# Attention and a max-out feed-forward on one core: the head of the loop's table in another order

## The chip, the cores and the metric

The kernel runs on one core of a Trainium2 chip. A core has five engines that work side by side, each with a queue that it goes through in order: TensorE (PE in the profile, with PEld for its weight loads), VectorE (DVE), ScalarE (ACT), GpSimd (POOL) and SyncE (SP), which here only issues DMAs. The metric is the device time of one execution in microseconds (us), as the median of several runs. Before the change it is 288.52 us.

## What is computed

```python
scores = scale * (q @ k_all.T)        # k_all: 16 beacon keys, then 576 keys; per batch and head
scores = where(causal, -1e9, scores)  # beacons are always seen
a = exp(scores - max); a /= a.sum(-1) + 1e-9
x = (a @ v_all), heads side by side   # 8 batches x 576 tokens = 4608 rows of 512
h = maximum(maximum(x @ w1, x @ w2), x @ w3)   # 512 -> 768
out = h @ w_out                                # 768 -> 512
```

There are 8 batches and 8 heads of width 64. Inputs and outputs are float32; the kernel computes its matmuls in bfloat16.

## The kernel before

**The work.** Heads go in pairs: pair p (0 to 31) is two heads of batch p // 4. Two pairs are a quad (0 to 15), and a half of a quad's 288 queries is one step of values. For a pair, q and k are loaded in float32 (a stage "st", one of eight), cast to bfloat16 (`cast`, tile p16), and turned so that the head dimension lies on the partitions (qT and kT, six of each). Pairs 10 to 13 are turned by PE (`pair`: twelve matmuls of line 393 into PSUM, then DVE moves kT, line 459, and ACT or DVE moves qT, line 448, in this order). Pairs from 14 on are turned by a transposing DMA (`cross`, line 374, on SP's queue). `keys` puts the 16 beacon keys in front of kT (line 455).

A pair's scores are four groups (0 to 3) of matmuls (line 509), each in one PSUM place of two banks. ACT takes the exp of a group into the tile at_sb (line 524), and `mask` sets what the causal order forbids to zero: on POOL with a select (line 543), on DVE with a product by a triangle (line 541). `("scores", p, g, n)` emits matmuls and exp, with n spare matmuls on constants first (line 473, 320 columns each); `("score", p, g)` emits the matmuls alone and `("exp", p, g)` the exp later.

`values` of a quad and a half multiplies the exps by ones (the sums) and by V (line 584) into two banks. `invert` is Ln and Exp on ACT (lines 604 and 606), and `multiply` is three products on DVE (line 616) into xT. V is loaded by batch in two pieces and cast by POOL (`cast v`, line 311).

The feed-forward is a list of units in order: for each block of 512 tokens 18 units of four matmuls (lines 646, or 665 for halves of block 0) with a cast or max by DVE (lines 654, 656, 673, 675), then four units of six matmuls for the output (line 682) that DVE copies to y (line 694). `("ffn 1", bank)` emits the next unit into a bank, `("ffn 2",)` the next two into a place of the ring.

**PSUM.** Eight banks: pv0 and pv1, one bank each, and a ring of three places of two banks, two called sc and one called wide. Each user of the ring (a group of scores, values "ring", "ffn 2", "ffn 1" with "ring", a pair that PE turns) takes the next place in turn, and PE has to wait until the user three turns ago has been read by DVE or ACT.

**The order.** Nothing is scheduled by a planner: two tables, `first_steps` and `loop_steps`, list the steps, and each engine does its part of them in the table's order. The loop's head works on pairs 8 to 13 (values 3 to 5) and on the end of block 0 and block 1 of the feed-forward. `("load", n)` issues the next n loads of a list (after pair 15: V of batch 3 in two pieces, the beacon keys of batches 4 to 7, pairs 16 to 19, V of batch 4, and so on); with an engine's name, that engine first writes one element of the stage, so that the load waits for its place in that engine's queue. `late` gives up the tiles of the start and sets up the nine y tiles. The change touches the table `loop_steps` alone. What a bank's name means to `values` is decided so:

```python
banks = None
if bank == "ring": ...      # values(): the next ring place
elif bank == "ffn": ...     # two ffn banks
else:                       # any other name
    banks = [pv_bank(i, [128, 512], FP32) for i in range(2)]
```

Of the kernel before, what the change touches and what calls it, by code (L numbers as in the profile page):

```python
# [16 lines left out]
def kernel(  # L17
# [141 lines left out]
    ring = [(sc_psum, "sc"), (sc_psum, "sc")]  # L159
# [684 lines left out]
    def start_late():  # L844
# [226 lines left out]
        ("mask", 6, 2, "pool"),  # L1071
    ]
    loop_steps = [
        ("late",),
        ("ffn 1", "pv1"),
        ("scores", 8, 1, 0),
        ("scores", 8, 0, 0),
        ("score", 8, 2),
        ("values", 3, 0, "pv"),
        ("invert",),  # L1080
        ("exp", 8, 2),
        ("values", 3, 1, "ring"),
        ("mask", 8, 1, "pool"),
        ("mask", 8, 0, "pool"),
        ("mask", 8, 2, "pool"),
        ("multiply",),
        ("invert",),
        ("multiply",),
        ("ffn 2",),
        ("ffn 1", "pv0"),  # L1090
        ("cast", 10, "pool", "pool"),
        ("load", 1),
        ("ffn 1", "pv1"),
        ("ffn 1", "pv0"),
        ("scores", 8, 3, 0),
        ("scores", 9, 0, 0),
        ("scores", 9, 1, 0),
        ("mask", 8, 3, "pool"),
        ("mask", 9, 0, "pool"),
        ("mask", 9, 1, "pool"),  # L1100
        ("ffn 1", "pv1"),
        ("ffn 1", "pv0"),
        ("pair", 10, "act"),
        ("keys", 10, "act"),
        ("ffn 2",),
        ("ffn 1", "pv1"),
        ("cast", 11, "pool", "pool"),
        ("load", 1),
        ("cast v", 2, 0),
        ("load", 1),  # L1110
        ("scores", 9, 2, 0),
        ("scores", 9, 3, 0),
        ("mask", 9, 2, "pool"),
        ("mask", 9, 3, "pool"),
        ("ffn 1", "pv0"),
        ("ffn 1", "pv1"),
        ("pair", 11, "act"),
        ("keys", 11, "act"),
        ("ffn 1", "pv0"),
        ("cast v", 2, 1),  # L1120
        ("load", 1),
        ("ffn 1", "pv1"),
        ("scores", 10, 1, 0),
        ("scores", 10, 0, 0),
        ("score", 10, 2),
        ("values", 4, 0, "pv"),
        ("invert",),
        ("exp", 10, 2),
        ("values", 4, 1, "ring"),
        ("mask", 10, 1, "pool"),  # L1130
        ("mask", 10, 0, "pool"),
        ("mask", 10, 2, "pool"),
        ("multiply",),
        ("invert",),
        ("multiply",),
        ("ffn 2",),
        ("ffn 1", "pv0"),
        ("cast", 12, "pool", "pool"),
        ("load", 1),
        ("cast", 14, "pool", "pool"),  # L1140
        ("load", 1),
        ("ffn 1", "pv1"),
        ("scores", 10, 3, 0),
        ("scores", 11, 0, 0),
        ("scores", 11, 1, 0),
        ("mask", 10, 3, "pool"),
        ("mask", 11, 0, "pool"),
        ("mask", 11, 1, "pool"),
        ("ffn 1", "pv0"),
        ("cast keys 2", "pool"),  # L1150
        ("cross", 14, 0),
        ("cross", 14, 1),
        ("cast", 15, "pool", "pool"),
        ("load", 1),
        ("pair", 12, "act"),
        ("keys", 12, "act"),
        ("ffn 2",),
        ("ffn 1", "pv1"),
        ("cast", 13, "pool", "pool"),
        ("load", 1),  # L1160
        ("scores", 11, 2, 0),
        ("scores", 11, 3, 0),
        ("mask", 11, 2, "pool"),
# [14 lines left out]
        ("values", 5, 1, "ring"),  # L1178
        ("mask", 12, 1, "pool"),
        ("mask", 12, 0, "pool"),  # L1180
        ("mask", 12, 2, "pool"),
        ("multiply",),
        ("invert",),
# [2 lines left out]
        ("ffn 1", "pv0"),  # L1186
        ("cast", 16, "pool", "pool"),
        ("ffn 1", "pv1"),
        ("scores", 12, 3, 0),
        ("scores", 13, 0, 0),  # L1190
        ("scores", 13, 1, 0),
# [478 lines left out]
```

## Time and profile before

| what | us |
|---|---|
| median of 3 runs (lowest to highest) | 288.52 (288.41 to 289.38) |
| the profiled execution, its own time | 288.88 |
| its span, first to last instruction | 287.1 |
| busy: PE, DVE, ACT, POOL | 278.4, 169.7, 143.8, 121.6 |

The granted TensorE clock is 0.997 of full speed over the span. A row of a time line gives the start in us, the length in us, the engine, the kernel's line, the operation, output tile <- input tiles with shapes, and xN for N instructions taken together; in square brackets stands how long the engine had been idle and what ended that. A row of the groups by shape gives, behind the bar, the busy time in us and the mean time of one in ns, then the idle time before them. A row of the table of stretches gives the stretch, its length, and the busy time of PE, PEld, DVE, ACT and POOL with their instructions, the granted clock, the share of the DMA engines and GB/s. Matmuls overlap, so a matmul's length is longer than its step to the next.

### The profile page before, as it was taken

The numbers are of one execution on the slowest core, as the hardware profiler recorded it, in microseconds if no ns is written. First come the engines' busy times: TensorE is split into PE (matmuls) and PEld (weight loads), VectorE is DVE, ScalarE is ACT, GpSimd is POOL, SyncE is SP. The second block draws the span as 40 slices with busy tenths as digits, with TensorE's granted clock in tenths as the row PEclk, the third lists the DMA queues.
The fourth block names the chain that finished last, engine by engine and source line by source line (L and its number), as shares of the span: only waits on it lengthen the run. The fifth ranks groups of instructions, "written<-read, shape, count | busy, mean of one in ns | idle before, by whom it ended". The sixth has DMA issues, their size and how long they took to land.

```text
span 287.1 us, 8822 instructions
## 1 busy us (share of the span) xinstructions
PE 278.4 (97%) x3706; PEld 160.2 (56%) x3731; DVE 169.7 (59%) x317; ACT 143.8 (50%) x242; POOL 121.6 (42%) x252
## 2 busy tenths in 40 slices
PE   8999999999999999999999999999999999999994
PEld 7656777754646454545456787445544545444442
DVE  2456878766575657465745755567466655373372
ACT  3876676835647564736483268444853452201200
POOL 4562327736484584737376446653633230000000
PEclk9999999999999999999999999999999999999998
DMA  8999998999999987999999989999983003002104
GB/s 154 174 166 209 222 245 158 244 204 211 191 158 159 172 118 134 195 176 184 184 229 191 194 170 221 222 168 177 189 323 123 2 2 148 0 0 107 41 0 147
DMA packets 118231, 45.30 MB, mean 158 GB/s; under 512 B 107312, under 2 KB 112944, under 8 KB 118192
## 3 DMA queue, kind: packets, MB, share of 16 engines
q1 hardware_dynamic: 111984, 39.20, 74.7%
q0 software_dynamic: 5648, 5.21, 11.8%
q8 instruction: 29, 0.48, 0.7%
q10 hardware_dynamic: 560, 0.33, 0.5%
q14 instruction: 10, 0.08, 0.1%
HBM read 35.13 MB, written 9.44 MB: 155 GB/s over the span
## 4 chain that ended last, share of the span: by engine, by line
PE 89%; ACT 3%; DMA 2%; DVE 2%; POOL 1%; issue 1%; ACTq 0%; POOLq 0%
PE pv L646 21%; PE sc L646 15%; PE wide L646 8%; PE pv L682 6%; PE sc L509 6%; PE sc L682 5%; PE wide L682 4%; PE pv L584 4%; PE wide L584 4%; PE sc L584 4%; DMA quad<-in_k_dram 2%; PE wide L509 2%; ACT at_sb L524 2%; PE pv L473 2%; PE sc L665 1%; PE pv L665 1%
## 5 line engine op out<-in xcount | busy, mean ns | idle before, releaser
L524 ACT ACTIVATE at_sb<-sc 128x736 bf16<-128x736 f32 (+5 forms) x95 | 79.4, 868 | 59.2 <-PE sc L509 58.6
L543 POOL TENSOR_SCALAR_AFFINE_SELECT at_sb<-at_sb 128x256 bf16<-128x256 bf16 (+2 forms) x143 | 52.4, 385 | 109.3 <-ACT at_sb L524 101.2
L646 PEld LDWEIGHTS <-w_sb 128*128 128x128 bf16 x648 | 61.1, 98 | 60.7 <-issue 4.9
L646 PE MATMUL pv<-xT,w_sb 128*128 128x512 bf16 (+1 forms) x315 | 65.3, 347 | 0.3
L646 PE MATMUL sc<-xT,w_sb 128*128 128x512 bf16 (+1 forms) x205 | 45.6, 363 | 0.7 <-issue 0.2
L656 DVE TENSOR_TENSOR hT<-hT,pv 128x512 bf16<-128x512 bf16 x48 | 32.4, 686 | 13.2 <-PE pv L646 13.2
L524 ACT ACTIVATE at_sb<-wide 128x736 bf16<-128x736 f32 (+3 forms) x33 | 27.7, 840 | 23.6 <-PE wide L509 23.5
L255 POOL CAST p<-st 96x768 bf16<-96x768 f32 x48 | 38.2, 825 | 0.0
L682 PEld LDWEIGHTS <-hT 128*128 128x128 bf16 x210 | 19.5, 98 | 23.5 <-issue 1.1
L616 DVE TENSOR_TENSOR xT<-pv,recip 128x288 bf16<-128x288 f32 (+2 forms) x48 | 14.2, 351 | 26.4 <-ACT recip L606 26.3
L509 PE MATMUL sc<-qT,kT 64*128 64x288 bf16 (+6 forms) x298 | 27.8, 277 | 1.6 <-DVE kT L443 0.7
L656 DVE TENSOR_TENSOR hT<-hT,sc 128x1024 bf16<-128x1024 bf16 (+1 forms) x19 | 20.8, 1104 | 12.6 <-PE sc L646 12.5
L509 PEld LDWEIGHTS <-kT 64*128 64x128 bf16 x400 | 14.6, 94 | 20.8 <-issue 13.0
L584 PEld LDWEIGHTS <-v_sb 128*32 128x32 bf16 (+1 forms) x1408 | 24.8, 96 | 1.7 <-issue 0.6
L646 PE MATMUL wide<-xT,w_sb 128*128 128x512 bf16 (+1 forms) x110 | 24.5, 364 | 0.1
L682 PE MATMUL pv<-w_out_sb,hT 128*128 128x512 bf16 x83 | 19.9, 380 | 0.1
L311 POOL CAST v_sb<-st 128x1536 bf16<-128x1536 f32 (+2 forms) x21 | 18.4, 897 | 0.0
L654 DVE CAST hT<-pv 128x512 bf16<-128x512 f32 x20 | 13.7, 688 | 5.0 <-PE pv L646 5.0
L682 PE MATMUL sc<-w_out_sb,hT 128*128 128x512 bf16 x68 | 16.3, 380 | 0.2
L665 PEld LDWEIGHTS <-w_sb 128*128 128x128 bf16 x144 | 13.0, 98 | 3.4 <-issue 1.4
L606 ACT ACTIVATE recip<-lnd 128x288 f32<-128x288 f32 x32 | 14.2, 443 | 1.0
L694 DVE COPY y<-pv 128x512 f32<-128x512 f32 x14 | 9.7, 692 | 8.4 <-PE pv L682 8.1
(119 smaller groups left out, 278.8 us busy)
## 6 DMA issues: line engine op xcount, KB each, us to landing
st<-in_q_dram SPq DMA_DIRECT2D x24, 288.0 KB, 5.2
st<-in_k_dram SPq DMA_DIRECT2D x24, 288.0 KB, 6.3
st<-in_v_dram SPq DMA_DIRECT2D x24, 256.0 KB, 5.5
out_dram<-y SPq DMA_DIRECT2D x9, 512.0 KB, 3.8
out_dram<-y SPq DMA_DIRECT2D x17, 256.0 KB, 4.1
w_sb<-in_moe_w_dram POOLq DMA_DIRECT2D x6, 384.0 KB, 8.7
st<-in_v_dram SPq DMA_DIRECT2D x8, 224.0 KB, 4.9
st<-in_v_dram SPq DMA_DIRECT2D x8, 160.0 KB, 4.8
```

The costliest lines, as they stand in the source:

```text
L255: cast(t16.rearrange("p r h d -> p h r d"), st[0:QP, i * NQ2 : (i + 1) * NQ2].rearrange("p (h r d) -> p h r d", h=2, r=QR),)
L311: cast(v_sb[0:n, t:t1].rearrange("p t h d -> p (t h d)"), st[0:n, (t - t_lo) * H * D : (t1 - t_lo) * H * D],)
L509: nc.tensor.matmul(ps[:, e, off : off + q1 - q0], kT[hs, 128 * t : 128 * t + 128], qT[hs, q0:q1], start=True, stop=True, tile_position=(64 ...
L524: nc.scalar.activation(out=both_heads(p, gi), in_=ps[:, :, 0 : g_width(p, gi)], func=AF.Exp, scale=scale)
L543: nc.gpsimd.affine_select(out=view, in_=view, compare_op=ALU.is_ge, fill=0.0, base=x0, pattern=[[0, 2], [1, hi - lo]], channel_multiplier=-1,)
L584: nc.tensor.matmul(ps[bank][32 * j : 32 * j + 32, lo + q0 - qa : lo + qb - qa], lhsT, at_view(PPQ * quad + j // 2, t, j % 2, q0, qb), star ...
L606: nc.scalar.activation(out=recip, in_=lnd, func=AF.Exp, scale=-1.0)
L616: nc.vector.tensor_mul(xT[:, 2 * g + part - 1, c0 + ca : c0 + cb], ps[bank][:, lo : lo + cb - ca], recip[:, ca:cb],)
L646: nc.tensor.matmul(dst[:, o0 : o0 + n], w_in[i][:, ct, 128 * (ft + f) : 128 * (ft + f + 1)], xT[:, ct, x0 : x0 + n], start=(ct == 0), stop ...
L656: nc.vector.tensor_max(h, h, ps)
L665: nc.tensor.matmul(ps[:, f], w_in[i][:, ct, 128 * (ft + f) : 128 * (ft + f + 1)], xT[:, ct, tb * TOKB + lo : tb * TOKB + hi], start=(ct == 0),
L682: nc.tensor.matmul(ps[:, t - tt] if two else ps, hT[:, ft, 128 * t : 128 * (t + 1)], w_out_sb[:, ft, :], start=(ft == 0), stop=(ft == n_ft ...
```

## The change

Only rows of `loop_steps` change. No step is added or dropped, except for spare matmuls. The rows from the loop's start to scores 11 2 are in another order:

- Scores 8 1 get four spare matmuls ahead, and the matmuls of group 2 of pair 8 come ahead of group 0. Values 3 0 get the name "ring+". `late` comes after values 3 and the second `invert`.
- Casts 10 and v 2 0 come ahead of the masks of pair 8. Casts 12 and 11 are done by DVE (q) and ACT (k), cast 14 by ACT (q) and POOL (k), cast keys 2 by ACT; they were POOL's. Keys 11 go from ACT to DVE.
- Masks 8 0, 8 3, 10 0, 10 2 and 11 0 go from POOL to DVE.
- Three units of block 1 go from pv banks to the ring; the units stand at other places between the scores. Scores 9 3 come ahead of 9 2, and the transposes of pair 11 come one unit after them.
- Invert of values 4 1 and cast 14 come ahead of the exp of 10 2.
- The loads of pairs 16 to 19 and of one piece of V of batch 4 come later; three loads get an engine that writes an element first.

The first rows and the later ones, shortened:

```diff
-        ("late",),
         ("ffn 1", "pv1"),
-        ("scores", 8, 1, 0),
+        ("scores", 8, 1, 4),
+        ("score", 8, 2),
         ("scores", 8, 0, 0),
-        ("score", 8, 2),
-        ("values", 3, 0, "pv"),
+        ("values", 3, 0, "ring+"),
         ("invert",),
         ("exp", 8, 2),
         ("values", 3, 1, "ring"),
+        ("multiply",),
+        ("invert",),
+        ("late",),
+        ("cast", 10, "pool", "pool"),
+        ("cast v", 2, 0),
+        ("multiply",),
         ("mask", 8, 1, "pool"),
-        ("mask", 8, 0, "pool"),
+        ("mask", 8, 0, "dve"),
         ("mask", 8, 2, "pool"),
...
         ("ffn 2",),
+        ("ffn 1", "pv1"),
+        ("ffn 1", "pv0"),
         ("scores", 8, 3, 0),
+        ("mask", 8, 3, "dve"),
         ("scores", 9, 0, 0),
         ("scores", 9, 1, 0),
+        ("ffn 1", "pv1"),
+        ("cast", 12, "dve", "act"),
+        ("mask", 9, 1, "pool"),
+        ("ffn 1", "pv0"),
+        ("ffn 1", "ring"),
+        ("load", 1, "pool"),
+        ("cast", 11, "dve", "act"),
+        ("pair", 10, "act"),
+        ("keys", 11, "dve"),
+        ("mask", 9, 0, "pool"),
+        ("load", 1, "pool"),
+        ("ffn 1", "pv0"),
+        ("ffn 2",),
+        ("scores", 9, 3, 0),
+        ("scores", 9, 2, 0),
+        ("keys", 10, "act"),
+        ("mask", 9, 2, "pool"),
+        ("ffn 1", "pv0"),
+        ("pair", 11, "act"),
+        ("ffn 1", "ring"),
+        ("mask", 9, 3, "pool"),
+        ("ffn 1", "ring"),
+        ("ffn 1", "pv1"),
         ("cast v", 2, 1),
-        ("load", 1),
-        ("ffn 1", "pv1"),
         ("scores", 10, 1, 0),
         ("scores", 10, 0, 0),
         ("score", 10, 2),
         ("values", 4, 0, "pv"),
         ("invert",),
+        ("mask", 10, 0, "dve"),
+        ("values", 4, 1, "ring"),
+        ("multiply",),
+        ("invert",),
+        ("multiply",),
+        ("mask", 10, 1, "pool"),
+        ("load", 1),
+        ("cast", 14, "act", "pool"),
         ("exp", 10, 2),
+        ("ffn 2",),
+        ("ffn 1", "pv0"),
         ("ffn 1", "pv1"),
         ("scores", 10, 3, 0),
         ("scores", 11, 0, 0),
         ("scores", 11, 1, 0),
+        ("cross", 14, 0),
+        ("mask", 11, 1, "pool"),
+        ("mask", 11, 0, "dve"),
         ("mask", 10, 3, "pool"),
+        ("ffn 1", "pv0"),
+        ("mask", 10, 2, "dve"),
+        ("cast", 15, "pool", "pool"),
+        ("load", 1),
         ("cross", 14, 1),
         ("pair", 12, "act"),
         ("keys", 12, "act"),
         ("ffn 2",),
         ("ffn 1", "pv1"),
         ("cast", 13, "pool", "pool"),
         ("load", 1),
+        ("load", 1, "dve"),
+        ("cast keys 2", "act"),
         ("scores", 11, 2, 0),
         ("scores", 11, 3, 0),
...
         ("mask", 12, 0, "pool"),
+        ("load", 1),
         ("mask", 12, 2, "pool"),
...
         ("cast", 16, "pool", "pool"),
         ("ffn 1", "pv1"),
+        ("load", 1, "pool"),
```

More of the change, by code (lines that the diff above doesn't have):

```diff
@@ L1082 @@
         ("values", 3, 1, "ring"),
-        ("mask", 8, 1, "pool"),
-        ("mask", 8, 0, "pool"),
-        ("mask", 8, 2, "pool"),
         ("multiply",),
         ("invert",),
+        ("late",),
+        ("cast", 10, "pool", "pool"),
+        ("cast v", 2, 0),
         ("multiply",),
+        ("mask", 8, 1, "pool"),
+        ("mask", 8, 0, "dve"),
+        ("mask", 8, 2, "pool"),
         ("ffn 2",),
-        ("ffn 1", "pv0"),
-        ("cast", 10, "pool", "pool"),
-        ("load", 1),
         ("ffn 1", "pv1"),
@@ L1095 @@
         ("scores", 8, 3, 0),
+        ("mask", 8, 3, "dve"),
         ("scores", 9, 0, 0),
         ("scores", 9, 1, 0),
-        ("mask", 8, 3, "pool"),
-        ("mask", 9, 0, "pool"),
-        ("mask", 9, 1, "pool"),
-        ("ffn 1", "pv1"),
[L1102 to L1105, printed above, removed]
-        ("ffn 1", "pv1"),
[L1107 to L1119, printed above, removed]
+        ("ffn 1", "pv1"),
[7 more added lines that the diff above has]
+        ("keys", 11, "dve"),
+        ("mask", 9, 0, "pool"),
+        ("load", 1, "pool"),
[10 more added lines that the diff above has]
+        ("ffn 1", "ring"),
+        ("ffn 1", "pv1"),
         ("cast v", 2, 1),
-        ("load", 1),
-        ("ffn 1", "pv1"),
         ("scores", 10, 1, 0),
@@ L1127 @@
         ("invert",),
-        ("exp", 10, 2),
+        ("mask", 10, 0, "dve"),
         ("values", 4, 1, "ring"),
-        ("mask", 10, 1, "pool"),
-        ("mask", 10, 0, "pool"),
-        ("mask", 10, 2, "pool"),
         ("multiply",),
@@ L1135 @@
         ("multiply",),
+        ("mask", 10, 1, "pool"),
+        ("load", 1),
+        ("cast", 14, "act", "pool"),
+        ("exp", 10, 2),
         ("ffn 2",),
         ("ffn 1", "pv0"),
[L1138 to L1141, printed above, removed]
         ("ffn 1", "pv1"),
@@ L1145 @@
         ("scores", 11, 1, 0),
+        ("cross", 14, 0),
+        ("mask", 11, 1, "pool"),
+        ("mask", 11, 0, "dve"),
         ("mask", 10, 3, "pool"),
-        ("mask", 11, 0, "pool"),
-        ("mask", 11, 1, "pool"),
         ("ffn 1", "pv0"),
-        ("cast keys 2", "pool"),
-        ("cross", 14, 0),
-        ("cross", 14, 1),
+        ("mask", 10, 2, "dve"),
         ("cast", 15, "pool", "pool"),
         ("load", 1),
+        ("cross", 14, 1),
         ("pair", 12, "act"),
```

## The prediction

> **What bounds the kernel now.** I read the page first, for the share of each engine, then the table of stretches, the list of waits on TensorE (PE), and last the time lines of PE, ScalarE (ACT), VectorE (DVE) and GpSimd (POOL) through the loop's head, which starts near 55 us.
>
> ```profile
> span 287.1 us, 8822 instructions
> PE 278.4 (97%) x3706; PEld 160.2 (56%) x3731; DVE 169.7 (59%) x317; ACT 143.8 (50%) x242; POOL 121.6 (42%) x252
> ...
> 58.00:75.00 17.00, 16.89 (x144) 8.18 (x137) 11.92 (x20) 7.01 (x13) 8.38 (x15) 1.00 1.12 202
> 75.00:90.00 15.00, 14.89 (x216) 8.13 (x214) 9.37 (x17) 9.34 (x16) 10.35 (x19) 1.00 1.05 177
> ...
> PE pv L473 <- DVE busy L139: 1.3, 1, 1.3
> ```
>
> PE is busy 97% of the span. In the two stretches that the edited rows cover, it is busy 31.78 of 32 us at a granted clock of 1.00, and the longest wait that the list gives it, 1.3 us, lies at the very start. So TensorE bounds this part, and every microsecond that it waits in the head moves the end by the same amount: nothing behind it has slack to take it back. DVE, ACT and POOL have time to spare, but each has a queue in order, and each frees PSUM places that PE needs.
>
> The edited rows leave the loop's matmuls as they are, with one addition. So a gain can come only from a wait of PE that goes. This is the head:
>
> ```profile
> 54.23 0.88 DVE L616 TENSOR_TENSOR xT<-wide,recip 128x288 bf16<-128x288 f32 x3
> 55.02 1.27 DVE L675 TENSOR_TENSOR hT<-hT,pv 128x512 bf16<-128x512 bf16 x2
> ...
> 55.20 0.33 PE L509 MATMUL wide<-qT,kT 64*128 64x288 bf16 x4
> 55.37 0.57 PE L509 MATMUL sc<-qT,kT 64*128 64x288 bf16 x6
> 55.87 0.41 PE L584 MATMUL pv<-at_sb,ones 128*32 128x288 bf16 x12
> 56.35 0.63 PE L584 MATMUL pv<-at_sb,v_sb 128*32 128x288 bf16 x31
> ...
> 58.43 2.76 PE L682 MATMUL sc<-w_out_sb,hT 128*128 128x512 bf16 x11
> ...
> 75.32 0.40 PE L584 MATMUL pv<-at_sb,ones 128*32 128x288 bf16 x12
> 75.56 0.62 PE L584 MATMUL pv<-at_sb,v_sb 128*32 128x288 bf16 x32
> ```
>
> From the ones part of values 3 to its values part PE takes 0.48 us (55.87 to 56.35); the same step takes 0.24 us one round later (75.32 to 75.56). The difference, **0.24 us**, is a wait for bank pv1, which the second max of line 675 frees at 56.29. That is all that the head can give back.
>
> **The change, part by part.** *Four spare matmuls* stand ahead of scores 8 1 ("scores", 8, 1, 4). Seven of them took 1.05 us from their start to the next scores:
>
> ```profile
> 24.42 1.12 PE L473 MATMUL sc<-busy 128*128 128x320 bf16 x7
> 25.47 0.49 PE L509 MATMUL sc<-qT,kT 64*128 64x288 bf16 x8
> ```
>
> Less the 0.1 us that PE spends on going over to the scores' half rows, this is 0.14 us each, so 0.55 us for four. They write the "wide" place, which the multiplies of line 616 free at 55.11, so they run from about 55.16 to 55.71, and scores 8 1 start near 55.80 where they started at 55.20: **0.60 us later**. Values 3 then start at 56.47, after pv1 is free, and the old wait of 0.24 us is gone. Until here the balance is +0.36 us, and PE would be ready for the output products (line 682) at 58.79.
>
> *"score", 8, 2 ahead of "scores", 8, 0.* PSUM for scores is a ring of three places. Before, scores 8 1, 8 0, 8 2 and values 3 1 took wide, sc, sc, wide, and the output products took the place of 8 0. Now that place is the one of 8 2, and the exp of 8 2 comes last on ACT:
>
> ```profile
> 55.63 0.78 ACT L524 ACTIVATE at_sb<-wide 128x736 bf16<-128x736 f32 x1 [0.54 <-PE wide L509]
> 56.31 0.99 ACT L524 ACTIVATE at_sb<-sc 128x992 bf16<-128x992 f32 x1
> 57.19 0.42 ACT L604 ACTIVATE lnd<-pv 128x288 f32<-128x288 f32 x1
> 57.64 0.45 ACT L606 ACTIVATE recip<-lnd 128x288 f32<-128x288 f32 x1
> 57.99 0.92 ACT L524 ACTIVATE at_sb<-sc 128x928 bf16<-128x928 f32 x1
> ```
>
> ACT works these five without a pause and in the same order in both kernels, so they only move by the 0.60 us: the exp of 8 2, which ended at 58.91, ends at 59.51, and the output products start at about 59.56 in place of 58.43. This is a **new wait of 0.77 us** (59.56 - 58.79); the balance is +1.13 us. Behind it in PE's queue stand all later matmuls.
>
> *Feed-forward units in the ring, pair 11 sooner.* Three units move from pv banks to the ring, and the transposes of pair 11 now follow a double unit, two scores and one unit. They take the ring place of that double unit.
>
> ```profile
> 67.44 1.89 PE L646 MATMUL wide<-xT,w_sb 128*128 128x512 bf16 x7
> 70.58 1.90 PE L646 MATMUL pv<-xT,w_sb 128*128 128x512 bf16 x8
> 69.38 1.23 DVE L654 CAST hT<-wide 128x1024 bf16<-128x1024 f32 x1 [0.89 <-PE wide L646]
> ```
>
> A double unit's place is free 3.17 us after its start (69.38 + 1.23 - 67.44); with 0.06 us for the signal, as at 56.29 to 56.35 above, 3.23. PE comes back to it after the same pieces that lie between the first two rows (the double unit, one unit, two scores), only in another order: 70.58 - 67.44 = 3.14 us. That is a wait of **0.09 us**; the balance is +1.22 us.
>
> *Casts and masks dealt anew.* Neither a cast of 96x768 by DVE or ACT nor masks between the loop's DVE work are in the trace. The nearest rows:
>
> ```profile
> L227 DVE CAST h<-h 96x384 bf16<-96x384 f32 x2 | 0.6, 352 | 3.8 <-DMA h<-in_k_dram 3.8
> L323 DVE CAST v_sb<-st 80x512 bf16<-80x512 f32 x1 | 0.4, 424 | 0.0
> L323 ACT CAST v_sb<-st 128x512 bf16<-128x512 f32 x3 | 1.9, 622 | 1.0 <-DVE hT L673 1.0
> L541 DVE TENSOR_TENSOR at_sb<-at_sb,tri 128x224 bf16<-128x224 bf16 x4 | 1.1, 266 | 0.7 <-ACT at_sb L524 0.7
> L255 POOL CAST p<-st 96x768 bf16<-96x768 f32 x48 | 38.2, 825 | 0.0
> ```
>
> For DVE's cast the ends are 0.35 us (half the columns) and 0.83 us (POOL's); the line through the two DVE rows gives 0.56 us, which I take. ACT's lies between 0.62 and 1.0 us; I take 0.85 us. ACT idles 9.99 of the 17 us from 58 on, which covers two of them; the one of pair 14 delays the exp of 10 2, but the scores that take its place come only behind a double unit and two single ones, over 3 us. On DVE, casts 12 and 11 and mask 8 3 are 1.4 us, with a small copy of keys, in a stretch where DVE idles 5.1 of 17 us; by my sum it has caught up by the double unit, and PE finds each pv bank free in time. At 0.83 us a cast, one bank comes 0.1 us late. A gain is excluded here, since PE waited for none of these. A mask takes 0.27 us where nothing is in its way. I cost the lot at nothing, and keep +0.1 us.
>
> *POOL's queue* now has casts 10 and v 2 0 ahead of masks 8 1 and 8 2; their reader, values 4, starts after 75.32. *SP's queue:* loads 16 to 19 go later, past a transposing DMA of pair 14, which waits for ACT's cast.
>
> ```profile
> st<-in_k_dram SPq DMA_DIRECT2D x24, 288.0 KB, 6.3
> ...
> 80.41 0.38 SPq L207 DMA_DIRECT2D st<-in_q_dram  x1
> ...
> 93.73 1.59 POOL L255 CAST p<-st 96x768 bf16<-96x768 f32 x2
> ```
>
> Load 16 is issued 13.3 us ahead of its cast and needs 6.3 us to land, so 7 us cover it: nothing. If that cover went, POOL's casts would wait, which they never did (0.0 in the row above).
>
> *Masks 11 0 and 10 2 on DVE* are the tightest place. Scores 11 3 need the ring place of pair 12, free once DVE has moved kT and then ACT qT:
>
> ```profile
> 82.16 1.67 ACT L524 ACTIVATE at_sb<-sc 128x992 bf16<-128x992 f32 x2
> 82.70 0.68 PE L393 MATMUL wide<-ident,p 96*128 96x96 bf16 x12
> 83.51 0.75 DVE L459 COPY kT<-wide 128x576 bf16<-128x576 bf16 x1
> 84.29 0.64 ACT L448 COPY qT<-wide 128x576 bf16<-128x576 bf16 x1 [0.47 <-DVE kT L459]
> 84.74 3.14 POOL L255 CAST p<-st 96x768 bf16<-96x768 f32 x4
> 86.11 0.31 PE L509 MATMUL wide<-qT,kT 64*128 64x336 bf16 x2
> ```
>
> Before, the place was free at 84.93, 1.18 us early. With +1.22 us scores 11 3 are due at 87.33. Mask 11 0 holds DVE's queue until the exp of 11 0 ends (82.16 + 0.99 + 1.22 = 84.37); then follow its two pieces (to 84.9), a max (0.64, half of the 1.27 above), mask 10 2 (0.27) and the kT move (0.75): 86.56 with no overlap, and the qT move ends at 87.24, 0.09 us early. It just fits.
>
> The sum for the profiled execution, 288.88 us around its span of 287.1, is 0.60 - 0.24 + 0.77 + 0.09 = +1.22 us: 290.10. The median of the runs shown is 288.52, 0.36 us lower; on it the forecast is **289.7 us**, +0.4%, which is within the 0.5% that a measurement of this kernel can tell from no change.
>
> **The rivals.** *Port (slower).* A DVE mask that meets a POOL cast waits for its end:
>
> ```profile
> 41.09 1.46 POOL L311 CAST v_sb<-st 128x1536 bf16<-128x1536 f32 x1
> 41.59 1.11 DVE L541 TENSOR_TENSOR at_sb<-at_sb,tri 128x256 bf16<-128x256 bf16 x1
> ```
>
> The mask took 1.11 us, not 0.27, and ended 0.15 us after the cast. Mask 10 2 is due on DVE at about 85.5, just as POOL reaches cast 15 after its own masks. Behind one piece of the cast (0.79 us, a quarter of 3.14) the qT move ends some 0.7 us late, behind both 1.5 us late, and PE stands at scores 11 3: 290.5 to 291.3 us, I say 290.9. It decides once DVE is held for more than 0.1 us there. For it: POOL's queue holds two masks and four casts in a row there. Against: the ops only collide if DVE comes second. The Trainium skill (SBUF — State Buffer, section "Who interferes with whom") states that DVE and GpSimd share one pair of ports as an exclusive lock, and that the later one blocks for the whole instruction. The two rows above agree; the price above is from the rows alone.
>
> *The wait at the output products does not come (no slower).* If their ring place is free in time, because I count the ring one place off or ACT comes sooner, +0.45 us is left: 289.0. Speaking against it, the trace names the places (wide, sc, sc, wide, sc) as I count them.
>
> *The spares are hidden (faster).* If PE waits there anyway, for longer than 0.55 us, the 0.24 us saved remain: 288.3 us. PE's step at 55.20 shows no such wait. Nor does "ring+" do anything: the helper of values treats all names but "ring" and "ffn" as the pv banks.
>
> **How the numbers follow.** Forecast 0.50 (289.3 to 290.2 us), port 0.30, no wait at the output products 0.16, spares hidden 0.04. Slower by over 0.5% means above 289.96: the port and a fifth of the forecast, 0.40. Faster by over 0.5% (below 287.1) lies beyond all that PE waits for in the head; I leave it half of the last rival, 0.02. The rest, 0.58, is within. The range goes from 288.6 to 291.2 us: it takes in the forecast, the second rival and most of the port.
>
> **What would show it.** Right: PE's output products near 59.5 after a gap of 0.8 us ended by ACT line 524; scores 8 1 at 55.8; values 3 without a break; values 4 near 76.5; every PE start after 110 us late by the same amount. Wrong: the output products start by 58.9; a DVE mask of over 0.5 us beside a POOL cast with a gap of PE at scores 11 3; PE waits for a load; or shifts that grow after 110 us.

## The result, and the profile after

The changed kernel takes **293.77 us** (292.96 to 294.61, 4 runs) where the kernel before takes 288.95 us (288.41 to 289.70, 4 runs) beside it. The medians are 4.82 us, or 1.7%, apart; the recorded ratio is 1.0149, interval 1.0122 to 1.0176. It is slower by some 1.5%, and 2.6 us above the top of the predicted range. Single executions of 405 to 716 us, which came with four of the kernels, that before among them, are disturbed: the medians given here include them, the ratios don't. The profiled execution took 294.15 us. Its page:

```profile
span 292.4 us, 8863 instructions
...
PE 282.0 (96%) x3735; PEld 160.6 (55%) x3735; DVE 176.7 (60%) x329; ACT 146.4 (50%) x245; POOL 114.2 (39%) x241
...
PEclk9999999999997999999999999999999999999999
```

The 7 in the clock's thirteenth slice (87.7 to 95.0 us) is new. The table of stretches puts the loss in the same place:

```profile
58.00:75.00 17.00, 17.00 (x176) 8.71 (x165) 13.78 (x25) 9.07 (x16) 5.27 (x12) 1.00 1.09 201
75.00:90.00 15.00, 12.19 (x190) 6.52 (x188) 11.78 (x19) 7.69 (x13) 4.86 (x8) 1.00 0.98 158
90.00:104.00 14.00, 13.87 (x190) 7.34 (x190) 7.47 (x15) 7.93 (x16) 4.08 (x10) 0.88 0.86 156
```

PE is idle for 2.8 us of the second stretch (busy 12.19 of 15.00, and 14.89 in the kernel before), and runs at a mean clock of 0.88 in the third. The list of waits has one new entry on PE in that stretch, and the time lines of DVE, POOL, ACT and PE around it show the chain:

```profile
PE wide L509 <- ACT qT L448: 2.9, 1, 2.9
```

```profile
84.51 0.68 DVE L656 TENSOR_TENSOR hT<-hT,pv 128x512 bf16<-128x512 bf16 x1
85.11 3.63 DVE L541 TENSOR_TENSOR at_sb<-at_sb,tri 128x256 bf16<-128x256 bf16 x1
88.66 0.74 DVE L459 COPY kT<-wide 128x576 bf16<-128x576 bf16 x1
...
84.83 0.68 POOL L543 TENSOR_SCALAR_AFFINE_SELECT at_sb<-at_sb 80x160 bf16<-80x160 bf16 x2 [6.86 <-ACT at_sb L524]
85.47 3.13 POOL L255 CAST p<-st 96x768 bf16<-96x768 f32 x4
...
89.44 0.64 ACT L448 COPY qT<-wide 128x576 bf16<-128x576 bf16 x1 [4.68 <-DVE kT L459]
...
86.82 0.37 PE L509 MATMUL sc<-qT,kT 64*128 64x464 bf16 x2
90.13 0.44 PE L509 MATMUL wide<-qT,kT 64*128 64x336 bf16 x2 [2.94 <-ACT qT L448]
90.50 2.74 PE L682 MATMUL pv<-w_out_sb,hT 128*128 128x512 bf16 x6
...
95.22 0.33 PE L509 MATMUL sc<-qT,kT 64*128 64x288 bf16 x4
```

Read from the second row. Mask 10 2 on DVE begins at 85.11, just as POOL's second select does, and it ends at 88.74: **3.63 us** where a mask takes 0.27. POOL's four cast pieces run from 85.47 to 88.60 without a gap, and the mask ends 0.14 us after the last. Behind the mask stands the kT move of pair 12, behind that ACT's qT move, and only then is the ring place free for scores 11 3, which start at 90.13. Then six output products take 2.74 us; they took 1.47 us in the kernel before.

That kernel's PE rows at the same six output products, at the first scores of pair 12 and at its last matmuls, and then two rows of the changed one, at values 4 and at its last matmuls:

```profile
86.34 1.47 PE L682 MATMUL pv<-w_out_sb,hT 128*128 128x512 bf16 x6
...
89.59 0.33 PE L509 MATMUL sc<-qT,kT 64*128 64x288 bf16 x4
...
281.98 1.47 PE L705 MATMUL pv<-w_out_sb,hT 128*128 128x320 bf16 x12
```

```profile
76.26 0.41 PE L584 MATMUL pv<-at_sb,ones 128*32 128x288 bf16 x12
...
287.60 1.47 PE L705 MATMUL pv<-w_out_sb,hT 128*128 128x320 bf16 x12
```

| PE step | before | after | later by | new since the row above |
|---|---|---|---|---|
| values 4 | 75.32 | 76.26 | 0.94 | 0.94 |
| scores 11 3 | 86.11 | 90.13 | 4.02 | 3.08: the wait |
| scores 12 1 | 89.59 | 95.22 | 5.63 | 1.61: the clock |
| last matmuls | 281.98 | 287.60 | 5.62 | nothing |

Of the 0.94 us, 0.16 were there at 48 us, ahead of every edited row, and 0.40 are a stop at 57 us that is treated at the end. So 0.38 us are left for the head, and 4.69 us come from one place. The span grew by 5.3, 0.3 less, because the work behind the last matmuls ended that much sooner.

### The profile page after: what moved, and what is told of

Same layout as the page of the kernel before. It is cut to its first block, busy times and chain, and to the rows that moved or that the text cites. A ratio compares the mean times of both kernels' runs of the same rounds, so it can differ in the third digit from the quotient of the medians.

```text
span 292.4 us, 8863 instructions
## 1 busy us (share of the span) xinstructions
PE 282.0 (96%) x3735; PEld 160.6 (55%) x3735; DVE 176.7 (60%) x329; ACT 146.4 (50%) x245; POOL 114.2 (39%) x241
## 4 chain that ended last, share of the span: by engine, by line
PE 88%; DMA 4%; ACT 3%; DVE 2%; issue 1%; POOL 1%; ACTq 0%
PE pv L646 19%; PE sc L646 16%; PE wide L646 7%; PE pv L682 7%; PE sc L509 6%; PE sc L682 5%; PE pv L584 5%; PE wide L682 4%; PE sc L584 4%; PE wide L584 4%; PE pv L665 3%; PE wide L509 3%; DMA quad<-in_k_dram 2%; ACT at_sb L524 2%; DMA bk<-in_beacon_k_dram 2%; PE sc L665 1%
## 5 line engine op out<-in xcount | busy, mean ns | idle before, releaser
L524 ACT ACTIVATE at_sb<-sc 128x992 bf16<-128x992 f32 (+5 forms) x94 | 78.6, 867 | 58.2 <-PE sc L509 57.6
L543 POOL TENSOR_SCALAR_AFFINE_SELECT at_sb<-at_sb 128x256 bf16<-128x256 bf16 (+2 forms) x135 | 49.2, 382 | 118.1 <-ACT at_sb L524 102.9
L646 PE MATMUL pv<-xT,w_sb 128*128 128x512 bf16 (+1 forms) x308 | 62.8, 346 | 0.0
L646 PE MATMUL sc<-xT,w_sb 128*128 128x512 bf16 (+1 forms) x232 | 50.3, 365 | 0.0
L524 ACT ACTIVATE at_sb<-wide 128x736 bf16<-128x736 f32 (+3 forms) x34 | 28.7, 843 | 23.2 <-PE wide L509 23.1
L656 DVE TENSOR_TENSOR hT<-hT,pv 128x512 bf16<-128x512 bf16 x46 | 31.0, 685 | 12.3 <-PE pv L646 12.3
L255 POOL CAST p<-st 96x768 bf16<-96x768 f32 x43 | 34.2, 822 | 0.1
L646 PE MATMUL wide<-xT,w_sb 128*128 128x512 bf16 (+1 forms) x108 | 23.7, 363 | 0.0
L682 PE MATMUL pv<-w_out_sb,hT 128*128 128x512 bf16 x84 | 21.3, 397 | 0.0
L541 DVE TENSOR_TENSOR at_sb<-at_sb,tri 128x256 bf16<-128x256 bf16 (+4 forms) x29 | 12.6, 469 | 3.6 <-ACT at_sb L524 3.6
```

Of the source, the lines that this page charges most:

```text
L255: cast(t16.rearrange("p r h d -> p h r d"), st[0:QP, i * NQ2 : (i + 1) * NQ2].rearrange("p (h r d) -> p h r d", h=2, r=QR),)
L524: nc.scalar.activation(out=both_heads(p, gi), in_=ps[:, :, 0 : g_width(p, gi)], func=AF.Exp, scale=scale)
L543: nc.gpsimd.affine_select(out=view, in_=view, compare_op=ALU.is_ge, fill=0.0, base=x0, pattern=[[0, 2], [1, hi - lo]], channel_multiplier=-1,)
L646: nc.tensor.matmul(dst[:, o0 : o0 + n], w_in[i][:, ct, 128 * (ft + f) : 128 * (ft + f + 1)], xT[:, ct, x0 : x0 + n], start=(ct == 0), stop ...
L656: nc.vector.tensor_max(h, h, ps)
L682: nc.tensor.matmul(ps[:, t - tt] if two else ps, hT[:, ft, 128 * t : 128 * (t + 1)], w_out_sb[:, ft, :], start=(ft == 0), stop=(ft == n_ft ...
```

## The experiments

**Theory:** mask 10 2, once it has lost POOL's port, waits for as long as POOL goes from one cast to the next, and the idle PE is then throttled; the rest of the change costs next to nothing. **Rivals:** the loss comes from what was moved on POOL's or SP's queue, and the mask only shows it; DVE is held for one instruction, and something else makes up the rest; the half clock costs nothing in the end.

**Mask 10 2 back on POOL**, at its new place:

```diff
-        ("mask", 10, 2, "dve"),
+        ("mask", 10, 2, "pool"),
```

> The changed kernel with mask 10 2 back on POOL, at the same place of the table. Theory (port): in the changed kernel this one DVE mask took 3.63 us because POOL works two masks and four casts without a pause, and PE lost 3.1 us at scores 11 3 and about 1.6 us at half clock after it; with the mask on POOL both go, about -4.7 us, so 289.1 us, and the kT move of pair 12 (line 459) starts near 85.2 in place of 88.66. Rival (queue): DVE simply has too much in its queue there, mask 11 0 with its wait for the exp above all; then only the 0.3 us of the mask itself goes, about 293.4 us.

Measured: 289.21 us, ratio 0.9996 (0.9979 to 1.0013). POOL and DVE:

```profile
85.79 1.04 POOL L543 TENSOR_SCALAR_AFFINE_SELECT at_sb<-at_sb 80x160 bf16<-80x160 bf16 x3 [6.86 <-ACT at_sb L524]
...
86.06 0.75 DVE L459 COPY kT<-wide 128x576 bf16<-128x576 bf16 x1
```

The kT move no longer has a mask ahead of it, and starts beside POOL's three selects. The whole loss is gone, with every other edit in place. The queues of POOL and SP are not the cause.

**The mask on DVE, one row sooner:**

```diff
+        ("mask", 10, 2, "dve"),
         ("mask", 11, 0, "dve"),
...
-        ("mask", 10, 2, "dve"),
```

> The changed kernel with mask 10 2 still on DVE, but one row ahead of mask 11 0 instead of behind the unit after it. DVE's work is the same to the instruction. Theory (port): DVE reaches it near 83 us, when POOL idles (77.97 to 84.83), so it takes 0.3 us, the wait of PE at scores 11 3 and the half clock go, about 289.1 us. Rival (queue): same work in the same stretch, so no change, about 293.8 us.

Measured: 289.38 us, 1.0001 (0.9989 to 1.0014).

```profile
82.46 0.28 DVE L541 TENSOR_TENSOR at_sb<-at_sb,tri 128x256 bf16<-128x256 bf16 x1
...
84.75 0.75 DVE L459 COPY kT<-wide 128x576 bf16<-128x576 bf16 x1
...
86.66 0.31 PE L509 MATMUL wide<-qT,kT 64*128 64x336 bf16 x2
```

The same instruction on the same engine takes 0.28 us, ahead of mask 11 0's wait for its exp. So it is not DVE that is wrong for this mask, but DVE at the moment when POOL begins a run of casts.

**The same mask moved alone in the kernel before**, first to a place that turned out about 1 us too soon:

```diff
-        ("mask", 10, 2, "pool"),
...
+        ("mask", 10, 2, "dve"),     # behind the unit after mask 11 1
```

> The kernel before with one edit: mask 10 2 goes to DVE and behind the unit that follows mask 11 1, where the changed kernel has it. Theory (port): POOL works without a pause from about 83.2 to 88.6 there, the mask lasts until about 88.6, scores 11 3 start near 90 in place of 86.1, and PE runs at half clock for some us after: +4 to +6 us, about 294 us. Rival (queue) and any theory that needs the other edits (loads, spares, casts on DVE): DVE has 0.3 us more to do, within 0.3 us of before, about 289.0 us.

Measured: 289.39 us, 1.0003 (0.9986 to 1.0019): **a miss**. I had counted on the mask meeting the casts.

```profile
83.10 0.28 DVE L541 TENSOR_TENSOR at_sb<-at_sb,tri 128x256 bf16<-128x256 bf16 x1
...
82.81 1.12 POOL L543 TENSOR_SCALAR_AFFINE_SELECT at_sb<-at_sb 128x224 bf16<-128x224 bf16 x3 [0.48 <-ACT at_sb L524]
83.88 0.60 POOL L895 CAST bk<-bk 64x512 bf16<-64x512 f32 x1
```

It came between two selects, and POOL, not DVE, paid: its three selects took 1.12 us (1.02 in the kernel before). Whether it costs 0.1 or 3.6 us is a matter of a microsecond in time. So the mask went to where the casts are:

```diff
-        ("mask", 10, 2, "pool"),
...
         ("keys", 12, "act"),
+        ("mask", 10, 2, "dve"),
```

> The kernel before with one edit: mask 10 2 goes to DVE behind the kT move of pair 12, near 84.3 us, when POOL is in the cast of the beacon keys with four pair casts right behind it (e3 put it a microsecond sooner, between two masks of POOL, where it took 0.28 us). Theory (port): it lasts until POOL's last cast ends near 87.9 or the masks behind it near 88.6, so 3.5 to 4.3 us; the max of units 15 and 16 waits behind it, the output products (line 682) of block 1 wait for that, about 3 us, and the clock may drop after it: +3 to +5 us, about 293 us. Rival (it takes the other edits of the change): 289.4 us.

Measured: 293.87 us, 1.0132 (1.0086 to 1.0178). Of its five undisturbed executions four took 293.12 to 294.84 us and one 290.63; that one has no profile.

```profile
85.05 3.85 DVE L541 TENSOR_TENSOR at_sb<-at_sb,tri 128x256 bf16<-128x256 bf16 x1
...
85.06 0.60 POOL L895 CAST bk<-bk 64x512 bf16<-64x512 f32 x1
85.61 3.14 POOL L255 CAST p<-st 96x768 bf16<-96x768 f32 x4
88.72 0.81 POOL L543 TENSOR_SCALAR_AFFINE_SELECT at_sb<-at_sb 128x256 bf16<-128x256 bf16 x2
```

```profile
PE pv L682 <- DVE hT L656: 2.0, 1, 2.0
```

DVE's mask begins 0.01 us ahead of POOL's first cast, while the last select still runs, and gets through after the fifth cast, at the step from cast to select. One row moved in the kernel before brings nearly the whole loss of the change; the wait on PE stands at another step, since here a max of the feed-forward is queued behind the mask.

**Fewer casts in a row, and a break between them.** The changed kernel was run again beside these:

> The changed kernel itself, beside the next three on one chip, as their yardstick: 293.8 us, and mask 10 2 again 3.6 us long.

Measured: 293.92 us, 1.0176 (1.0137 to 1.0216), and the mask takes 3.63 us again. Then cast 15 goes behind mask 11 3, which leaves two pieces on POOL at the place:

```diff
-        ("cast", 15, "pool", "pool"),
...
         ("mask", 11, 3, "pool"),
+        ("cast", 15, "pool", "pool"),
```

> The changed kernel with cast 15 behind mask 11 3, so that POOL's run at mask 10 2 holds two casts (pair 13) and not four. Theory (the mask waits for POOL's whole run of back-to-back work): the mask ends 1.6 us sooner and takes about 2.1 us, PE waits 1.5 us at scores 11 3 in place of 3.1, and so short a wait leaves the clock at 1.00: about 3.2 us less than the changed kernel, 290.6 us. Rival (the mask waits for one instruction and something else holds it 3.6 us): no change, 293.8 us.

Measured: 290.55 us, 1.0042 (1.0024 to 1.0060).

```profile
84.24 2.09 DVE L541 TENSOR_TENSOR at_sb<-at_sb,tri 128x256 bf16<-128x256 bf16 x1
...
84.59 1.59 POOL L255 CAST p<-st 96x768 bf16<-96x768 f32 x2
```

```profile
PE wide L509 <- ACT qT L448: 1.4, 1, 1.4
```

Two pieces less, 1.54 us less for the mask and 1.5 us less for PE; and the clock stays at 1.00. The next kernel leaves all four pieces and puts one instruction between the second and the third that writes SBUF and reads nothing (`busy` is read by the spare matmuls alone; the step is new):

```diff
         ("cast", 15, "pool", "pool"),
...
+        ("write only",),    # nc.gpsimd.memset(busy, 1.0)
         ("cast", 13, "pool", "pool"),
```

> The changed kernel with one POOL memset of 128x320 (it reads nothing of SBUF, and its 0.3 us of data is not used again) between cast 15 and cast 13. Theory A (a DVE op with two SBUF inputs gets in as soon as POOL works on something that does not read): the mask ends beside the memset, near 87.2, it takes about 2.1 us, PE waits some 1.6 us, clock 1.00: about 290.9 us. Theory B (it gets in only when POOL's queue pauses): the mask lasts 0.3 us longer, near 3.9 us, and the time is that of the changed kernel plus 0.3, about 294.1 us.

Measured: 290.89 us, 1.0049 (1.0030 to 1.0068).

```profile
84.28 2.08 DVE L541 TENSOR_TENSOR at_sb<-at_sb,tri 128x256 bf16<-128x256 bf16 x1
...
84.64 1.59 POOL L255 CAST p<-st 96x768 bf16<-96x768 f32 x2
86.17 0.37 POOL L853 MEMSET busy<- 128x320 bf16 x1
86.48 1.59 POOL L255 CAST p<-st 96x768 bf16<-96x768 f32 x2
```

POOL has more to do than in the changed kernel, and the kernel is 3.0 us faster, because DVE gets in at the memset. So what counts is neither POOL's total nor the number of casts queued, but how many casts POOL goes through without another instruction between them. The Trainium skill (SBUF — State Buffer, section "Who interferes with whom") states that a DVE instruction with two inputs in SBUF contends with GpSimd instructions that read SBUF and not with those that only write it: the memset agrees. It also states that the loser blocks for the whole instruction; here it stood behind four and five casts in a row, and the measurement decides. The memset's run doesn't show that writing alone is what matters: a select reads SBUF, and DVE got in ahead of one too, behind the fifth cast above.

**The half clock.** 20 spare matmuls into bank pv0 between scores 11 2 and 11 3 keep PE at work through its wait (`spare pv0` is a new step):

```diff
+        ("spare pv0", 20),
         ("scores", 11, 3, 0),
```

> The changed kernel with 20 spare matmuls of 320 columns into bank pv0 between scores 11 2 and 11 3, about 2.7 us that lie in the wait of 3.1 us. Theory: the wait for pair 12 stays (scores 11 3 near 90.1), but PE works on through it, so the granted clock stays 1.00 and output products (line 682) take 1.3 us and not 2.6: -1.6 us, about 292.2 us. Rival: the half clock has another cause than PE's idle time (the loads, the load of the whole chip); then no gain, 293.8 us or a little over.

Measured: 293.21 us, 1.0134 (1.0114 to 1.0154). Only 0.6 us came back where 1.6 were expected. Since the changed kernel had not run on that chip, the two were run together:

> The kernel with 20 spare matmuls in the wait at scores 11 3 again, now beside the changed kernel on the same chip. Theory (half clock behind the wait costs 1.6 us, and the spares take it away): 1.6 us below the changed kernel. Rival (the half clock is made up for elsewhere, or hardly any execution has it in full): 0.7 us or less below it, as the medians of two chips said.

> The changed kernel itself, for the comparison with the run that has spare matmuls in its wait: 293.8 us, 1.016 of the kernel before, with a clock of 0.5 for some 3.4 us behind the wait at scores 11 3.

Measured: 293.65 us with the spares, 1.0142 (1.0125 to 1.0159), and 293.53 us without, 1.0143 (1.0123 to 1.0164): **no gain in the total**, as the rival said. The time line of PE with the spares:

```profile
86.56 2.89 PE L473 MATMUL pv<-busy 128*128 128x320 bf16 x20
89.58 0.32 PE L509 MATMUL wide<-qT,kT 64*128 64x336 bf16 x2
89.83 1.47 PE L682 MATMUL pv<-w_out_sb,hT 128*128 128x512 bf16 x6
...
93.03 0.33 PE L509 MATMUL sc<-qT,kT 64*128 64x288 bf16 x4
...
183.13 1.04 PE L682 MATMUL sc<-w_out_sb,hT 128*128 128x512 bf16 x4 [0.79 <-issue]
```

From scores 11 3 to scores 12 1 PE takes 3.45 us, as in the kernel before (89.59 - 86.11 = 3.48), and 5.09 us in the changed kernel: at the place itself the spares save 1.64 us. About 0.96 us of it is lost again between two output products, at 181.95 to 183.13; in the other run with the spares the step between the same two instructions has 1.39 us too much. No semaphore ends that stop ("issue"), and none of the three profiles of the changed kernel has it. The rest is lost at another stop: near 57 us PE takes 0.88 us too long in the profile with the spares and nothing in that without them, run beside it. Together the two stops, 1.84 us, take back all of the 1.64. So the half clock costs 1.6 us where it happens, and spares in the wait don't make the total shorter. What the stops are, and whether every execution behind the medians has them, stays open.

**The spares of scores 8 1 taken out**, with the mask one row sooner as above:

```diff
-        ("scores", 8, 1, 4),
+        ("scores", 8, 1, 0),
```

> The changed kernel with mask 10 2 one row ahead of mask 11 0 (still on DVE) and scores 8 1 without their four spare matmuls. Theory (the spares cost PE 0.60 us less the old wait of 0.24 us for bank pv1, which comes back): 0.36 us below the kernel with the mask ahead and the spares in, which stood at 1.0001 of the kernel before, so some 289.0 us where the kernel before is at 289.4, ratio 0.9988. Rival (the spares lie beside a wait that is there anyway): ratio 1.000.

Measured: 289.20 us, 0.9992 (0.9977 to 1.0008). The interval holds both expectations. The trace says more:

```profile
56.27 0.41 PE L584 MATMUL pv<-at_sb,ones 128*32 128x288 bf16 x12
56.76 0.68 PE L584 MATMUL pv<-at_sb,v_sb 128*32 128x288 bf16 x27
```

Without the spares, the step from the ones part of values 3 to its values part is 0.49 us again, 0.25 us longer than the 0.24 of an undisturbed round. Against the changed kernel of the same chip, this trace is 0.86 us behind at 48 us, 0.24 at 56 and 0.63 at 64: the spares cost 0.62, and 0.39 comes back, 0.25 at this step and 0.14 among the matmuls of values 3 behind it. At 89 us it is 2.48 ahead and at 96 us 4.15, and so it stays to the last matmul: 3.11 us for the wait and 1.67 for the clock, with none of it given back here. No version found here is faster than the kernel before: with the mask put right, the change comes out even.

## Why the prediction was wrong

**The step that failed** is the last one of the working, "It just fits": it gives mask 10 2 0.27 us on DVE. It took 3.63 us, and scores 11 3 came 3.1 us late in place of none. The port rival named this mask, this place and this chain, and the point from which it decides (held over 0.1 us); what was mis-sized there is its price. "Behind one piece" 0.7 us and "behind both" 1.5 us (which on 289.7 give 290.4 and 291.2 us, 0.1 less than it says) took the end of cast 15's first or second piece as DVE's way in, though the rival itself counts four casts in a row. POOL's run was four pieces, and none of the boundaries between them let DVE in: a wait of some 1.5 us (1.4 in the list) is what the kernel with two pieces shows. The reason given against the rival, that DVE has to come second, was no reason: DVE's mask and a select of 0.40 us began in the same moment, 85.11, and the casts followed. The row on which the rival's price rested (a mask beside a single cast, behind which POOL then stood idle for 1.11 us) could not show a run of casts.

**A term that the sum did not have** is the clock. The table of the kernel before has 1.00 in every stretch but the last (0.98), and I read it as a constant. Its record of the clock does go to 0.50 at the end, from 285.56 us on, 2.1 us behind the last matmul. After a wait of 3.1 us PE ran at half clock: 2.74 us for six products that take 1.47, and 1.61 us lost. After waits of 1.4 us it did not.

**Step by step.** *The four spares:* scores 8 1 came 0.65 us after the spares' start (55.33 to 55.98), 0.64 predicted. *The old wait for pv1:* gone, as predicted; without the spares it is back at 0.25 us. *The balance up to the output products:* +0.36 predicted if nothing makes them wait. They start 0.94 us later (58.43 to 59.37); less the 0.16 from ahead and the stop's 0.40, 0.38 measured. Values 4 start 0.94 us later as well, so nothing came on top, where the sum had +1.22.

```profile
55.33 0.72 PE L473 MATMUL wide<-busy 128*128 128x320 bf16 x4
55.98 0.33 PE L509 MATMUL wide<-qT,kT 64*128 64x288 bf16 x4
...
57.28 0.20 PE L584 MATMUL pv<-at_sb,ones 128*32 128x48 bf16 x2 [0.23 <-issue]
...
59.37 2.76 PE L682 MATMUL sc<-w_out_sb,hT 128*128 128x512 bf16 x12
```

```profile
58.77 0.92 ACT L524 ACTIVATE at_sb<-sc 128x928 bf16<-128x928 f32 x1
```

*The new wait of 0.77 us* did not come. The output products began at 59.37, while the exp of 8 2 still read its place (58.77 to 59.69): they had another place, that of 8 0. The two scores were exchanged in the order of their matmuls, but the exp of 8 0 stands first in the table in both kernels, and its place went to the products in both. I had handed places out by the order of writers. The trace that I called on against this rival could not tell: two of the three places share the name sc. This is the rival "the wait doesn't come"; by it the head was 0.77 us cheaper than forecast. *The transposes of pair 11* predicted 0.09 us of wait; the balance, the same 0.94 us ahead of them and behind them, leaves no room for it that could be told from zero. *Casts:*

```profile
66.95 0.55 DVE L255 CAST p<-st 96x768 bf16<-96x768 f32 x1
...
67.18 1.57 ACT L255 CAST p<-st 96x768 bf16<-96x768 f32 x2
```

On DVE 0.55 us (0.56 taken), on ACT 0.79 (0.85 taken), and no one waited for them. Masks on DVE elsewhere met POOL too (mask 8 0 beside cast v 2 0), and it cost nothing, since nothing that PE waited for was queued behind them. *Loads and the queues of SP and POOL* cost nothing, as predicted (four loads, not three, have an engine that writes first): with only the mask moved back, the kernel stands at 0.9996.

So the forecast's +1.22 us was two errors of opposite sign beside a head that was right: 0.86 us of waits that did not come, and 4.7 us at the place that I had called the tightest and priced as fitting.

## What to carry to other kernels

Before an elementwise product of two SBUF tiles goes from POOL to DVE, look at what POOL does at that very time: price it by the whole unbroken run of POOL's casts, not by one of them, and look at what stands behind it in DVE's queue. A row earlier it can be free. When a wait on PE comes out at 2 to 3 us, price the clock as well: here it added half of the wait again. And the place of a ring that comes next has to be followed by the readers' order too: here, in the one case seen, it was not the writers' order that decided.

## What the runs showed of the hardware that I had not expected

**Who gets the port between two instructions.** DVE's waiting product got in where POOL went from a cast to a select (88.7 us in the kernel before with the mask in the casts), from one select to the next (83.1 us, where it hardly had to wait: 0.28 us) and from a cast to a memset (86.2 us). It did not get in from a select to a cast (85.5 us in the changed kernel) nor at any step from cast to cast (three there, four in the kernel before with the mask in the casts). Why a following cast keeps the port and a following select doesn't was not settled. A longer gap ahead of the select would explain it, but the profile doesn't show one.

**The clock.** The records of the granted clock have 0.50 from 90.20 to 93.62 us in the changed kernel, 3.41 us. Its two other profiles have 3.41 and 6.83 us, the latter in an execution of 297.21 us, and the kernel before with the mask in the casts has 3.41 after a wait of 2.0 us. With the spares in the wait, and behind waits of 1.4 us, there is none at this place. The Trainium skill (TensorE: Matmul & The Clock Gate, Part 1) gives a window of about 3.4 us that runs freely, with half rate after an idle one. The lengths of one and two times 3.4 us agree; the waits of 2.0 and 3.1 us that were enough do not, if the window must be wholly idle.

**Stops without a cause in the profile.** PE stops for 0.2 to 1.6 us at some instructions while nothing that it waits for is late. In three profiles of the changed kernel and its variants the stop near 57 us stands at the same pair of matmuls of values 3, with 0.40, 0.88 and 1.75 us too much. In the second of these, with the spares, the stops at 56 and 182 us come after instructions 1979 and 5552 of PE's stream, by the count of its records. That page also lists transfers of a kind of their own:

```profile
PE 282.7 (97%) x3755; PEld 161.7 (56%) x3755; DVE 176.1 (60%) x329; ACT 146.4 (50%) x245; POOL 114.7 (39%) x241
...
q8 instruction: 29, 0.48, 0.7%
```

7510 instructions of PE by 29 transfers are 259 each, and the two stops are 3573 apart, 13.8 times that. A stop at the edge of a loaded piece of code would ask for a whole number there; 13.8 is near one and no more, some records can be missing, and no run was made to test it. So the cause stays open. It is why a local saving, like that of the spares, has to be looked for again in the total.
